# Pooled attention and routed experts in one program: where a later batch's products, a split tile's sums and the last tiles' sums stand in the TensorE queue

## The chip, the cores and the metric

The kernel runs on one core of a Trainium2 chip. The metric is the time of one execution in microseconds, the median of three runs. Five engines work side by side, each through its own queue in program order: TensorE (PE, with its weight loads shown as PEld), VectorE (DVE), ScalarE (ACT), GpSimd (POOL) and SyncE (SP), which only issues transfers. A queue whose next instruction waits on a semaphore holds back all that stands behind it.

## The reference, cut to what matters

Eight batches of eight heads with 576 tokens of 64 numbers. Keys and values are averaged over groups of eight tokens, so that each query sees 72 pooled keys. The result, 4608 tokens of 512 numbers, goes to a router and eight experts; each expert takes exactly 576 tokens, in the order of the largest logits.

```python
k_p = k.reshape(B, H, Sp, pool, D).mean(axis=3)
v_p = v.reshape(B, H, Sp, pool, D).mean(axis=3)
scores = scale * np.matmul(q, k_p.transpose(0, 1, 3, 2))
attn = np.exp(scores - np.max(scores, axis=-1, keepdims=True))
attn = attn / (np.sum(attn, axis=-1, keepdims=True) + 1e-09)
out = np.matmul(attn, v_p)
...
logits = x @ w_gate
order = np.argsort(-logits.flatten())
for idx in order:                      # the first free expert that a token's logits lead to
    tok, e = (int(idx) // E, int(idx) % E)
    if assigned[tok] >= 0 or counts[e] >= cap: continue
    assigned[tok] = e; counts[e] += 1
...
out[mask] = np.maximum(x[mask] @ w1[e], 0.0) @ w2[e]
```

## The kernel before, in words

**Attention.** The 4608 tokens are 36 tiles of 128. Since a batch has 576 tokens, four and a half tiles, four tiles (4, 13, 22 and 31) are split: their two halves belong to two batches. The order of the instructions is the order in which the Python code is written; nothing moves them afterwards. The loop of `run` goes over n = 0 to 35 and works on three tiles at once:

- `st_s(n)`, L230: the scores of tile n into the PSUM tile `pss`, of which there is one (two banks).
- `st_e(n-1, g)`, L259 and L260: the exponentials `e` of tile n-1 are transposed on TensorE (three blocks for g = 0 into `pse`, two for g = 1 into `rt`), and ScalarE copies them to `eT`. `rt` is one single bank, shared with everything in `prep_v`, `prep_g` and the router.
- `st_av(n-2, g)`, L272: the products of `eT` with `vblk`, the pooled values laid out by heads, into one of two PSUM tiles `psa`. In one go they give, per head, 64 sums, eight logit parts (the value rows times the router's weights, put beside the values) and the sum of the exponentials: 73 columns. An unsplit tile has six instructions for g = 0 and four for g = 1 (each matmul of 32-bit numbers is two), a split one twelve and eight with half the columns of weights.
- `softmax(n)`, L240 to L242: maxima and subtraction on VectorE, the exponential on ScalarE.
- `norm(n-3)`, L293 to L306: reciprocals of the sums, the logits (for four tiles at a time, L299, when n-3 is the last of four), and the normalised rows `xt` on VectorE; ScalarE issues their store to `xd` in memory (L311).

GpSimd pools the keys and values of a later batch meanwhile (L175 to L198; `vsum` is written at L190). Before a batch's values can be used, `prep_v(b)` (L211, three transposes of `vsum` into `rt`, copied by ScalarE, L213) and `prep_g(b)` (L220, products with the router's weights into `rt`; VectorE writes them into `vblk`, L221) must run. They are planned in `at`, a table by n whose entries run at the end of an iteration, behind `norm`.

**The last tiles.** `finish` brings tiles 33 to 35 to their logits and starts the router: `after` is the generator `Routing.begin`, and each `next(after)` emits a piece of it between the attention's instructions. `st_av` is called with nine columns (the logits and the sum), and the 64 other columns are left to `st_x` (L281), whose twenty instructions for the last two tiles stand between the pieces of the router's search. `put_x` scales them on ScalarE (L348).

**The router.** `search` finds, in four rounds, the logit at which the first expert is full. A round compares (DVE, L631), counts on TensorE (36 small products, L636), decides on VectorE (L694) and spreads the decision (L701, L703). `close` then turns the choice into the rows of the first expert (L775), GpSimd gathers those rows (L1042, an indirect transfer), and the experts' stage begins. `warm` is a number of products of ones that nobody reads (L529). `wake` gathers 32 rows that nobody reads (L1188); one stands behind tile 30's `norm`, one in the last round of the search.

## Time and profile before

| | |
|---|---|
| median of 3 runs | 609.79 us (609.03 to 609.95) |
| the profiled execution | 609.97 us |
| its span on the chip | 608.2 us |
| mean granted TensorE clock | 0.977 |
| TensorE busy | 588.5 us, 97% of the span |
| VectorE, ScalarE, GpSimd busy | 394.1, 302.2, 175.6 us |
| attention loop | 8.6 us to 133.1 us |
| last tiles and router, up to the first gather | 133.1 us to 156.7 us |
| experts | from 160.1 us |

How to read it: times in the trace are microseconds from the start of the span. The chain that ended last is followed back from the last instruction, at each step to what released it, so what stands in it sets the end. "issue" in it is time in which an engine waited for nothing that the profile shows. In a timeline row stand the start, the duration, the engine, the line and the tiles; in brackets the idle time before it and what ended it. The granted clock is the TensorE clock as a share of full speed.

### The profile page before, as it was taken

What the parts mean: (1) busy time and instruction counts of PE and PEld (TensorE: products, weight loads), DVE (VectorE), ACT (ScalarE), POOL (GpSimd) and SP (SyncE); (2) the same over time, 40 slices, a digit from 0 to 9 for tenths busy, and PEclk for the clock granted to TensorE, in tenths of its full rate; (3) what the DMA queues carried; (4) which work ended last, traced back from release to release, by engine and by line L of the source; (5) the groups of instructions that cost most, each with busy time, mean ns of one, the idle gap of its engine ahead of it and who ended that gap; (6) DMA issues with size and microseconds to landing.
All of it is one profiled execution on the core that took longest, in us unless ns stands there. A gap on an engine that the chain in (4) does not pass through costs nothing.

```text
span 608.2 us, 11352 instructions
## 1 busy us (share of the span) xinstructions
PE 588.5 (97%) x4196; PEld 510.5 (84%) x4196; DVE 394.1 (65%) x1150; ACT 302.2 (50%) x621; POOL 175.6 (29%) x220
## 2 busy tenths in 40 slices
PE   8999999998899999999999999999999999999993
PEld 5999999987598779878977997898799889879972
DVE  7577777986796777867964886387567437506200
ACT  7444444442362275365764495267338627825210
POOL 2999999000300420221122211212121121220021
PEclk9999999995799999999999999999999999999998
DMA  9999972121550761557721942473085247313010
GB/s 356 420 423 401 420 267 86 72 87 37 160 197 1 233 173 72 190 134 224 207 71 52 337 80 62 161 242 92 36 300 134 61 162 240 87 60 148 3 57 27
DMA packets 63907, 99.87 MB, mean 164 GB/s; under 512 B 34753, under 2 KB 34785, under 8 KB 61153
## 3 DMA queue, kind: packets, MB, share of 16 engines
q1 hardware_dynamic: 52560, 70.66, 34.6%
q0 software_dynamic: 5952, 18.90, 9.1%
q10 hardware_dynamic: 5328, 9.48, 4.2%
q8 instruction: 35, 0.57, 0.4%
q14 instruction: 32, 0.25, 0.1%
HBM read 72.41 MB, written 18.87 MB: 150 GB/s over the span
## 4 chain that ended last, share of the span: by engine, by line
PE 84%; issue 8%; DVE 2%; ACT 2%; DMA 2%; POOL 1%; POOLq 0%; another core or an unknown queue 0%; ACTq 0%
PE h L1129 30%; PE h L1163 24%; PE psa L272 8%; PE pss L230 6%; PE h L1168 4%; PE pse L259 2%; PE rt L259 1%; DMA xg<-xd,rows 1%; PE rt L220 1%; PE rt L675 1%; PE rt L636 1%; PE rt L529 1%; DMA out_dram<-yt,rows 1%; POOL out_dram L1143 1%; PE rt L211 1%
## 5 line engine op out<-in xcount | busy, mean ns | idle before, releaser
L1163 PE MATMUL h<-w2l,hh 128*128 128x512 f32 x256 | 101.5, 397 | 0.0
L1163 PE MATMUL h<-w2h,hl 128*128 128x512 f32 x256 | 101.4, 396 | 0.0
L1163 PE MATMUL h<-w2h,hh 128*128 128x512 f32 x256 | 101.1, 395 | 0.3 <-PEq L1228 0.3
L1129 PE MATMUL h<-xl,w1h 128*128 128x256 f32 (+2 forms) x516 | 93.7, 300 | 0.0
L1134 ACT ACTIVATE hh<-h 128x256 fp32r<-128x256 f32 (+2 forms) x129 | 52.9, 411 | 81.7 <-PE h L1129 81.2
L1129 PE MATMUL h<-xh,w1h 128*128 128x256 f32 (+2 forms) x516 | 93.2, 299 | 0.2 <-ACT xh L1105 0.2
L1129 PE MATMUL h<-xh,w1l 128*128 128x256 f32 (+2 forms) x516 | 91.0, 297 | 0.5 <-DVE w1l L1083 0.5
L1143 POOL DMA_INDIRECT out_dram<-yt,rows x29 | 29.0, 999 | 185.7 <-ACT yt L1177 185.5
L1129 PEld LDWEIGHTS h<-xh,w1h 128*128 128x128 f32 x516 | 76.0, 189 | 3.3 <-issue 2.3
L1129 PEld LDWEIGHTS h<-xl,w1h 128*128 128x128 f32 x516 | 77.0, 190 | 0.1
L1129 PEld LDWEIGHTS h<-xh,w1l 128*128 128x128 f32 x516 | 76.1, 189 | 0.7 <-DVE w1l L1083 0.7
L1137 DVE SCALAR_TENSOR_TENSOR hl<-h,hh 128x256 fp32r<-128x256 f32 (+2 forms) x129 | 57.4, 448 | 25.6 <-ACT hr L1136 18.0
L1042 POOL DMA_INDIRECT xa<-xd,rows x33 | 32.6, 987 | 135.3 <-ACT xg L1059 51.4
L1177 ACT ACTIVATE yt<-h 128x512 f32<-128x512 f32 x32 | 19.2, 601 | 103.2 <-PE h L1163 72.6
L272 PE MATMUL psa<-vblk,eT 128*128 128x146 f32 (+5 forms) x400 | 61.9, 302 | 0.0
L1072 DVE TENSOR_TENSOR xl<-xg,xh 128x512 fp32r<-128x512 f32 (+1 forms) x33 | 20.7, 628 | 56.3 <-ACT xh L1071 56.2
L1163 PEld LDWEIGHTS h<-w2h,hh 128*128 128x128 f32 x256 | 48.2, 188 | 9.4 <-issue 0.7
L1163 PEld LDWEIGHTS h<-w2l,hh 128*128 128x128 f32 x256 | 48.3, 189 | 8.8
L1163 PEld LDWEIGHTS h<-w2h,hl 128*128 128x128 f32 x256 | 48.2, 188 | 8.8
L272 PEld LDWEIGHTS psa<-vblk,eT 128*128 128x128 f32 (+1 forms) x400 | 52.2, 182 | 1.7 <-POOL tk L175 0.3
L1083 DVE TENSOR_TENSOR w1l<-raw,w1h 128x512 fp32r<-128x512 f32 x64 | 41.4, 686 | 9.3 <-ACT w1h L1079 8.8
L1092 DVE TENSOR_TENSOR w2l<-raw,w2h 128x512 fp32r<-128x512 f32 x64 | 43.1, 680 | 2.8 <-ACT w2h L1089 2.7
(222 smaller groups left out, 962.4 us busy)
## 6 DMA issues: line engine op xcount, KB each, us to landing
raw<-in_moe_w_dram SPq DMA_DIRECT2D x64, 512.0 KB, 6.5
xd<-xt ACTq DMA_DIRECT2D x36, 256.0 KB, 4.6
rawv<-in_v_dram SPq DMA_DIRECT2D x7, 1280.0 KB, 13.9
rawk<-in_k_dram SPq DMA_DIRECT2D x7, 1152.0 KB, 13.1
rawq<-in_q_dram SPq DMA_DIRECT2D x7, 1152.0 KB, 11.6
rawk<-in_k_dram SPq DMA_DIRECT2D x2, 576.0 KB, 4.4
rawv<-in_v_dram SPq DMA_DIRECT2D x1, 768.0 KB, 7.8
rawq<-in_q_dram SPq DMA_DIRECT2D x1, 640.0 KB, 8.9
```

The lines of the kernel that those rows point to most:

```text
L230: nc.tensor.matmul(ps[cols, j // 2, 144 * (j % 2):144 * (j % 2) + 144], self.q_of(b, j, n, cols.stop - cols.start), self.kblk[b % 4][:, j] ...
L272: self.nc.tensor.matmul(o[h], self.eT[i][:, c, h], self.vblk[b % 4][:, self.BLOCKS[c]:self.BLOCKS[c + 1], cols], start=(c == cs[0]), stop= ...
L1042: self.nc.gpsimd.indirect_dma_start(out=to[:n], out_offset=None, in_=self.xd, in_offset=bass.IndirectOffsetOnAxis(ap=rows[:n, t:t + 1], ax ...
L1072: later(0.9, 0.7, lambda: self.nc.vector.tensor_tensor(xl, x, xh.bitcast(F32), op=OP.subtract))
L1083: self.nc.vector.tensor_tensor(l, raw, h.bitcast(F32), op=OP.subtract)
L1092: self.nc.vector.tensor_tensor(self.w2l[:, i], self.raw2[e][:, i], self.w2h[:, i].bitcast(F32), op=OP.subtract)
L1129: nc.tensor.matmul(ps[:, :m], a[:, j, fs], b[:, j, o], start=(n == 0), stop=(n == 11))
L1134: nc.scalar.activation(hh[:, f, o], ps[:, :m], AF.Relu)
L1137: later(0.65, 0.4, lambda f=f, o=o, m=m, ps=ps: nc.vector.scalar_tensor_tensor(hl[:, f, o], ps[:, :m], 0.0, hh[:, f, o].bitcast(F32), op0= ...
L1143: st = nc.gpsimd.indirect_dma_start(out=rows, out_offset=bass.IndirectOffsetOnAxis(ap=idx, axis=0), in_=y, in_offset=None)
L1163: nc.tensor.matmul(ps, a[:, f, o], b[:, f], start=(f == 0 and k == 0), stop=(f == 7 and k == 2))
L1168: nc.tensor.matmul(ps[64 * a:64 * a + 64, :256], self.hr[:, f], self.raw2[e][:, f, 256 * a:256 * a + 256], start=(f == 0), stop=(f == 7))
```

## The change

- `prep_v` and `prep_g` leave the table `at`. They are called directly behind `st_s(n)`, in the same iterations as before (`prep_v(b)` in n = first[b], `prep_g(b)` in the next; for batch 1 one iteration later each, n = 5 and 6).
- In an iteration whose `st_av` is of a split tile, both `st_e` come first and then both `st_av`. For unsplit tiles the order stays.
- `finish` computes the sums of the last two tiles whole, 73 columns, and `st_x` and `put_x` go. Tile 34's sums go into `pss` in place of `psa`, and their first part stands ahead of tile 35's transposes. The rows `xt` of tiles 33, 34 and 35 are all scaled on ScalarE at the end (24 instructions; before, 16, and one on VectorE for tile 33).
- The second `wake`, the three `warm` products in the first `close` and the last three double steps of `begin` go. What those steps emitted is now emitted by the experts' stage, with nothing of the attention between.

```diff
-    def st_av(self, i, g, cols=slice(0, 73)):
+    def st_av(self, i, g, bank=("psa", 2)):
         if g == 0:
-            self.pA[i] = self.ps.tile([128, 2, 512], F32, name="psa", bufs=2)
+            self.pA[i] = self.ps.tile([128, 2, 512], F32, name=bank[0], bufs=bank[1])
...
-        gate = slice(64, 73)
-        self.st_e(j, 0)
-        self.st_av(i, 0, gate)
-        self.st_e(j, 1)
-        self.st_av(i, 1, gate)
-        self.norm(i - 1)
+        self.st_av(i, 0, ("pss", 1))
+        for g in range(2):
+            self.st_e(j, g)
+        self.st_av(i, 1)
+        rinv = {i - 1: self.gates(i - 1, i - 1, i)}
         next(after)
...
+        for g in range(2):
+            self.st_av(j, g)
+        for t in (i, j):
+            if t == j:
+                next(after)
+            rinv[t] = self.gates(t, t, t + 1)
+            next(after)
+        for t in (i - 1, i, j):
+            ps = self.sums_of(t)
+            xt = self.wk.tile([128, 8, 64], F32, name="xt", bufs=8)
+            for h in range(8):
+                self.nc.scalar.activation(xt[:, h], ps[:, h, :64], AF.Copy, scale=rinv[t][:, h:h + 1])
+            self.store(t, xt)
...
-            plan(first[b] + (b == 1), self.prep_v, b)
-            if b > 1:
-                plan(first[b] + 1, self.prep_g, b)
+            behind[first[b] + (b == 1)] = lambda b=b: self.prep_v(b)
+            behind[first[b] + 1 + (b == 1)] = lambda b=b: self.prep_g(b)
...
-            if n >= 1:
-                self.st_e(n - 1, 0)
-            if n == first[1] + 2:
-                self.prep_g(1)
-            if n >= 2:
-                self.st_av(n - 2, 0)
-            if n >= 1:
-                self.st_e(n - 1, 1)
+            if n in behind:
+                behind[n]()
+            e = [lambda g=g: self.st_e(n - 1, g) for g in range(2 if n >= 1 else 0)]
+            av = [lambda g=g: self.st_av(n - 2, g) for g in range(2 if n >= 2 else 0)]
+            if n >= 2 and len(self.parts(n - 2)) == 1:
+                e[1:1] = av[:1]
+                av = av[1:]
             if n == 1:
-                self.prep_v(0)
-            if n >= 2:
-                self.st_av(n - 2, 1)
+                e.append(lambda: self.prep_v(0))
+            for f in (*e, *av):
+                f()
             self.softmax(n)
...
-                if not spare:
-                    self.wake()
...
-        if not k:
-            self.warm(3)
...
         self.best(self.NC - 1, self.NC)
         next(g)
         yield
-        for _ in range(3):
-            next(g)
-            next(g)
-            yield
```

On TensorE, in the iterations n = 9 and 10, where batch 2 is prepared (a row is the line, the instruction, the tile written and those read; `x2` means two such instructions in a row):

```order
 L259 MATMUL rt<-ident,e 127x128 x2
 L272 MATMUL psa<-vblk_178,eT_172 128x2x73 x2
-L211 MATMUL rt<-ident,vsum 128x128 x3
 L230 MATMUL pss<-kblk_132,rawq 128x144 x4
+L220 MATMUL rt<-wblk,vT 128x40
+L220 MATMUL rt<-wblk,vT 128x32
+L220 MATMUL rt<-wblk,vT 128x16
 L259 MATMUL pse<-ident,e 127x128 x3
```

The transposes of `vsum` no longer stand between the last sums of iteration 9 and the scores of tile 10 (they now stand behind tile 9's scores, one iteration's length earlier), and the products with the router's weights stand right behind tile 10's scores.

On TensorE, around the split tile 13 (iteration n = 15, the first rows are the end of n = 14):

```order
 L259 MATMUL rt<-ident,e 127x128 x2
 L272 MATMUL psa<-vblk_179,eT_171 128x2x73 x2
-L220 MATMUL rt<-wblk,vT 128x40
-L220 MATMUL rt<-wblk,vT 128x32
-L220 MATMUL rt<-wblk,vT 128x16
 L230 MATMUL pss<-kblk_133,rawq 128x144 x4
 L259 MATMUL pse<-ident,e 127x128 x3
+L259 MATMUL rt<-ident,e 127x128 x2
 L272 MATMUL psa<-vblk_179,eT_172 64x2x73
 L272 MATMUL psa<-vblk_180,eT_172 64x2x73
```

The second pair of transposes, which stood behind the first twelve products of the split tile, moves ahead of them, so that all twenty products stand in a row.

On TensorE, behind the loop. Before, with nine columns per head:

```order
L272 MATMUL psa<-vblk_180,eT_171 128x2x73 x2
L259 MATMUL pse<-ident,e 127x128 x3
L272 MATMUL psa<-vblk_180,eT_172 128x2x9
L272 MATMUL psa<-vblk_180,eT_172 128x3x9
L272 MATMUL psa<-vblk_180,eT_172 128x2x9
L259 MATMUL rt<-ident,e 127x128 x2
L272 MATMUL psa<-vblk_180,eT_172 128x2x9 x2
L272 MATMUL psa<-vblk_180,eT_173 128x2x9
L272 MATMUL psa<-vblk_180,eT_173 128x3x9
L272 MATMUL psa<-vblk_180,eT_173 128x2x9 x3
```

and with the change:

```order
L272 MATMUL psa<-vblk_180,eT_171 128x2x73 x2
L272 MATMUL pss<-vblk_180,eT_172 128x2x73
L272 MATMUL pss<-vblk_180,eT_172 128x3x73
L272 MATMUL pss<-vblk_180,eT_172 128x2x73
L259 MATMUL pse<-ident,e 127x128 x3
L259 MATMUL rt<-ident,e 127x128 x2
L272 MATMUL pss<-vblk_180,eT_172 128x2x73 x2
L272 MATMUL psa<-vblk_180,eT_173 128x2x73
L272 MATMUL psa<-vblk_180,eT_173 128x3x73
L272 MATMUL psa<-vblk_180,eT_173 128x2x73 x3
```

Here `eT_172` is tile 34 and `eT_173` tile 35. The first products of tile 34 move ahead of tile 35's transposes and into `pss`, and all have 73 columns per head; the rows of L281, which followed between the counting products, are gone.

## The prediction

> **What bounds the kernel now.** I read the chain that ended last first: TensorE holds 84% of it, and through the attention loop it runs from one TensorE group to the next almost without a gap. A group of products that takes less time on TensorE there therefore moves the end. Rows of the chain (start, duration, what), around the preparation of batch 3 and the split tile 13, with one row of batch 1 and one of an ordinary iteration:

> ```profile
> PE 84%; issue 8%; DVE 2%; ACT 2%; DMA 2%; POOL 1%; POOLq 0%; another core or an unknown queue 0%; ACTq 0%
> ...
> 25.11 0.98 PE pss L230 x8
> ...
> 29.98 0.58 PE rt L220 x6
> ...
> 49.80 1.10 PE pss L230 x8
> ...
> 56.11 0.12 issue
> 56.23 0.52 PE rt L211 x3
> 56.75 0.98 PE pss L230 x8
> 57.73 0.33 PE pse L259 x3
> 58.06 0.87 PE psa L272 x6
> 58.94 0.22 PE rt L259 x2
> 59.16 0.50 PE psa L272 x4
> 59.66 0.03 issue
> 59.69 0.84 PE rt L220 x6
> 60.53 1.08 PE pss L230 x8
> ...
> 62.96 0.42 PE rt L259 x2
> ```

> The reader is to see two prices of the same work. Three transposes cost 0.33 us where nothing is in their way (L259) and 0.12 + 0.52 us for `prep_v` (L211); six products with the router's weights cost 0.58 us in batch 1 and 0.03 + 0.84 us in batch 3. Both stand right behind `st_e(n-1, 1)`, whose bank `rt` they need: they wait for ScalarE's copy of it and then pay the pipeline's start.

> Behind the loop the path changes hands between TensorE and VectorE. Timeline rows of the last tiles and of the router's four rounds:

> ```profile
> 133.66 0.60 PE L259 MATMUL pse<-ident,e 128*127 128x128 f32 x3 [0.60 <-ACT e L242]
> ...
> 134.54 0.68 DVE L306 TENSOR_TENSOR xt<-psa,rinv 128x512 f32<-128x512 f32 x1
> ...
> 134.99 2.18 PE L272 MATMUL psa<-vblk,eT 128*128 128x18 f32 x14
> ...
> 135.25 0.38 ACT L260 ACTIVATE eT<-rt 127x256 f32<-127x256 f32 x1 [0.36 <-PE rt L259]
> ...
> 137.21 0.21 DVE L293 RECIPROCAL rinv<-psa 128x8 f32<-128x8 f32 x1
> ...
> 138.26 1.86 PE L281 MATMUL pss<-vblk,eT 128*128 128x128 f32 x6
> ...
> 138.52 0.22 DVE L631 TENSOR_TENSOR cmp<-q16a,j 128x128 bf16<-128x128 f16 x1
> ...
> 140.05 0.29 PE L636 MATMUL rt<-oh,cmp 128*32 128x8 bf16 x4
> ...
> 141.29 0.90 DVE L631 TENSOR_TENSOR cmp<-q,j 128x256 bf16<-128x256 f16 x3
> ...
> 141.85 1.75 ACT L348 ACTIVATE xt<-pss,rinv 128x64 f32<-128x64 f32 x8 [6.22 <-DVE cmp L631]
> ...
> 142.17 1.36 PE L636 MATMUL rt<-oh,cmp 128*32 128x8 bf16 x36
> ...
> 144.47 0.89 DVE L631 TENSOR_TENSOR cmp<-q,j 128x256 bf16<-128x256 f16 x3
> ...
> 145.57 1.36 PE L636 MATMUL rt<-oh,cmp 128*32 128x8 bf16 x36
> ...
> 147.86 0.90 DVE L631 TENSOR_TENSOR cmp<-q,j 128x256 bf16<-128x256 f16 x3
> ...
> 148.20 1.36 PE L636 MATMUL rt<-oh,cmp 128*32 128x8 bf16 x36 [0.23 <-DVE cmp L631]
> ```

> Counting (L636) starts 0.34 us after the comparison where nothing stands between (147.86 to 148.20), but 0.88 us after it in the second round, 1.10 us in the third, and the first round's last count waits until L281 is through, though its comparison ended at 138.74.

> **The change part by part.** *Preparation behind the scores.* Behind `st_s(n)` the bank `rt` has long been copied, and ScalarE copies `vT` while TensorE goes on with `st_e(n-1, 0)` and `st_av`. I take 0.33 us for the transposes and 0.58 us for the products, as in the rows. Before, they cost 0.12 + 0.52 + 0.03 + 0.84 = 1.51 us, less 0.12 us since scores behind `prep_v` take 0.98 us and not 1.10. The gain is 1.39 - 0.91 = 0.48 us a batch, 2.9 us for batches 2 to 7. The bounds: nothing, if the pipeline's start is paid at the new place, and 3.5 us.

> Two things are given back. The products end in a VectorE instruction (L221) that now stands ahead of tile n's maxima:

> ```profile
> 25.56 0.86 POOL L190 TENSOR_TENSOR vsum<-t 128x320 f32<-128x320 f32 x1
> ...
> 44.03 0.76 DVE L240 TENSOR_REDUCE mx<-pss 128x8 f32<-128x576 f32 x1 [0.96 <-PE pss L230]
> ...
> 46.60 0.68 DVE L306 TENSOR_TENSOR xt<-psa,rinv 128x512 f32<-128x512 f32 x1
> ...
> 47.20 0.24 DVE L221 TENSOR_TENSOR vblk<-rt,mask 128x88 f32<-128x88 f32 x1
> ```

> From the maxima's start to the end of `xt` VectorE needs 3.25 us in an iteration that also sums four tiles' logits (n = 10 here, and n = 14). The maxima would start 0.58 + 0.07 + 0.24 = 0.89 us after the scores, so `xt` ends 4.1 us after them. TensorE wants that `psa` at 0.58 + 0.33 + 0.87 + 0.22 + 0.50 + 1.10 + 0.33 = 3.9 us. It waits 0.2 us in batches 2 and 3; in batch 7, where the router's first pieces load VectorE too, I allow as much: 0.6 us in all. The exponentials themselves are not late: maxima, subtraction and ScalarE take about 2.4 us from the maxima's start, so they are there at 3.3 us against 3.6 us. If that margin is gone, a batch loses what it gained (rival B). And in batch 1 `vsum` is done at 26.42 us, while tile 5's scores end at 26.09 us: 0.33 us lost against the 0.12 us saved, 0.2 us.

> *Sums of a split tile in a row.* In iteration 15 the second transposes cost 0.42 us between two runs of half-width products, 0.22 us otherwise. In the new order TensorE changes between the widths once less: 0.20 us in four iterations, 0.8 us. The loop gives 2.9 + 0.8 - 0.6 - 0.2 = 2.9 us.

> *Whole sums of the last tiles.* The loop's last products end at 133.07 us, and TensorE then idles 0.60 us for tile 35's exponentials. With `pss` free (its last reader, the subtraction, is done before the exponential), tile 34's first part fills that time: 0.87 us to 133.94, transposes 0.33 + 0.22, then 0.50 + 0.87 + 0.50 us: 136.4 us. Before, the fourteen narrow products ended at 137.17. So whole sums are not later, at full clock; VectorE saves tile 33's `xt` (0.68 us) as well and could reach tile 35's reciprocal at 136.5. But a new wait stands there: `rinv` has two buffers, and the third one wanted (tile 35's) must wait until ScalarE has scaled tile 33 out of the first. ScalarE copies transposes until about 135.3 (0.3 us sooner than the row at 135.25 plus 0.38), and eight scalings take 1.75 us: 137.1 us, against 137.21 before. From there to the end of the comparison are 1.53 us (137.21 to 138.74), so counting starts near 138.7 and not at 140.05: 1.4 us. Bounds: 0.5 us, if the sums run at half clock, and 1.8 us without the wait. Behind the reciprocal are queued everything of VectorE's search, so that wait is on the path.

> *No products between the counts.* The second and third round lose 0.88 - 0.34 = 0.54 us and 1.10 - 0.34 = 0.76 us: 1.3 us gained. The fourth has no such gap. The sums' 24 scalings take 5.3 us of ScalarE, from 135.3 to about 141, and the last store starts then, long before the gather.

> *Wake and warm products.* These rows carry them, the next point and the rivals:

> ```profile
> 134.00:136.00 2.00, 2.00 (x21) 2.00 (x19) 1.90 (x9) 0.88 (x2) 0.00 (x0) 0.97 0.35 131
> 158.00:160.00 2.00, 1.58 (x4) 0.30 (x2) 1.96 (x4) 1.12 (x2) 1.70 (x2) 0.55 0.68 164
> ...
> 149.41 0.88 POOL L1188 DMA_INDIRECT norow<-in_moe_w_dram,noindex  x1 [41.48 <-DVE noindex L534]
> ...
> 155.15 4.43 PE L529 MATMUL h<-ones 128*128 128x512 bf16 x10
> ...
> 156.67 0.98 POOL L1042 DMA_INDIRECT xg<-xd,rows  x1 [6.38 <-issue]
> ```

> The second wake came after 41.48 us of idle GpSimd and took 0.88 us, less than the gather's 0.98: no sign of a queue gone cold, so I cost its removal at nothing, between -0.7 us (the gather may start sooner) and +0.9 us (it starts that much later again than its rows). The three warm products ran while TensorE waited for VectorE; they cost nothing.

> *Sum.* 2.9 + 1.4 + 1.3 = 5.6 us. The expert stage behind the gather keeps its order and moves whole. 609.97 - 5.6 = 604.4 us in terms of the profiled execution, which lay 0.18 us above the median: **604.2 us**.

> **The clock.** The window rows (columns: window, length, busy time of PE, PEld, DVE, ACT, POOL, then granted clock) show the clock at half from 135.9 (0.97 over 134 to 136) to 159.8 (0.55 over 158 to 160), 23.9 us. The ten warm products brought it back just before the gathered rows came. Shifted by 5.6 us they run from 149.55 to 154.0 us. [...]

> **The rivals.** *A, the forecast*, 604.2 us, 0.50.

> *B, the loop gives nothing*: VectorE's delayed maxima make TensorE wait for what it saves. For it: VectorE is busy three quarters of the loop. Against: 0.3 us of margin above. Only 2.7 us remain: 607.1 us, 0.15.

> [...] Price: 2 to 3.4 us at half clock, 1.0 to 1.7 us: 605.5 us, 0.14.

> *D, better*: the gather loses its 0.7 us of delay and the first counts run before the clock falls: 602.8 us, 0.09.

> *E, the other side*: without the three warm products the clock stays at half through the first expert's pieces. Place: TensorE from 154 us on. Price: half of the time spent so. It decides from 6.8 us lost (5.6 plus what can be told), 13.6 us at half clock: 611.0 us. For it: the half clock lasted 23.9 us with TensorE mostly busy. Against: ten warm products alone brought it back. 0.07. [...]

> *F, a cold GpSimd queue*: the gather pays what the second wake took on itself, its 0.88 us, a landing like the gather's 3.3 us, and 0.9 us of late start, 5.1 us: 609.3 us, 0.05. Against it stands the row at 149.41. [...]

> **How the numbers follow.** A measurement here tells 0.2%, 1.2 us, from no change. A, B, C and D are faster (0.88), F the same (0.05), E slower (0.07). The range leaves out E, F and a little of A and B: the low end is D with 1 us more from the loop's bounds (2.9 to 3.5 us and the new wait's 0.4), 601.8; the high end B with half a microsecond of late gather, 607.6.

> **What would show it.** Right: L211 and L220 with about 0.33 and 0.58 us in the chain and no "issue" ahead of them; the loop's last products ending near 130.2; VectorE's last reciprocal waiting for ScalarE; L636 starting 0.34 us after each comparison; the gather near 151. Wrong: DVE or ACT ahead of L230 or L272 in the chain of the loop (B); half clock beyond 154 (C, E); the gather more than 1 us behind its rows (F).

## The result, and the profile after

The changed kernel takes 603.46 us (median of 4 runs, 603.16 to 603.46), against 609.41 us for the kernel before on the same chip (608.62 to 609.95). The ratio is 0.9895, 95% interval 0.9882 to 0.9908. The forecast was 604.2 us with a range of 601.8 to 607.6, faster with 0.88. The profiled execution after took 603.46 us with a span of 601.6 us, 6.5 us less than the profiled one before.

The page of the kernel after, shares of the chain that ended last by engine:

```profile
PE 80%; issue 7%; DVE 5%; DMA 2%; ACT 2%; POOL 1%; POOLq 0%; another core or an unknown queue 0%; SPq 0%; ACTq 0%; DVEq 0%
```

TensorE lost four points of the path, VectorE gained three: part of the loop is now bound by VectorE.

To size the loop without its first tiles, take VectorE's row maxima, one instruction a tile, as mile marks. Timeline of the kernel before, the maxima of tiles 7 and 35 (start, duration, engine, line, instruction):

```profile
34.33 0.76 DVE L240 TENSOR_REDUCE mx<-pss 128x8 f32<-128x576 f32 x1 [0.34 <-PE pss L230]
...
131.07 0.74 DVE L240 TENSOR_REDUCE mx<-pss 128x8 f32<-128x576 f32 x1
```

The same two marks of the kernel after:

```profile
34.39 0.76 DVE L240 TENSOR_REDUCE mx<-pss 128x8 f32<-128x576 f32 x1
...
127.53 0.74 DVE L240 TENSOR_REDUCE mx<-pss 128x8 f32<-128x576 f32 x1
```

Between the marks lie 96.74 us before and 93.14 us after: the loop gave **3.60 us**. From tile 35's maxima to the first gather the time fell from 25.60 to 22.73 us, **2.87 us**. What lies ahead of tile 7 cost 0.06 us, and the rest of the span, with what lies around it, gave 0.1 us: 6.5 us in all. Eight profiles of kernels with the changed loop read 93.10 to 93.26 us between the marks, so differences of a few tenths mean something there.

The chain of waits of the kernel after, around the preparation of batches 2 and 3 and the split tile 13 (start, duration, what):

```profile
43.75 0.57 PE rt L220 x6
44.32 0.44 PE pse L259 x3
...
44.85 0.50 ACT eT L260
...
45.38 0.76 DVE e L241
...
47.18 0.61 DVE xt L297
...
47.92 1.11 PE psa L272 x6
...
53.83 0.48 PE rt L211 x3
...
57.22 0.57 PE rt L220 x6
57.79 0.43 PE pse L259 x3
...
61.24 0.22 PE rt L259 x2
61.46 1.52 PE psa L272 x20
```

The reader is to see three things. The products (L220) cost 0.57 us and no "issue" stands ahead of them, as forecast; the group behind them pays 0.10 us of it back (0.43 against 0.33 us), which the forecast had left out. In batch 2 the path leaves TensorE over the exponential and VectorE and returns with `xt`, whose bank the sums wait for: the give-back that the forecast named. In batch 3 nothing of the kind stands there. The split tile's twenty products run in one piece of 1.52 us behind transposes of 0.22 us (1.02 and 0.65 us in two pieces before, with the 0.42 us between them).

What the bank has to do with it can be read from the products' waits. Kernel before, batches 2 to 7, the products of L220:

```profile
L220 PE MATMUL rt<-wblk,vT x36: 262/276/303, 46.0 to 122.9; 128*128 128x40 f32 x12, 128*128 128x32 f32 x12, 128*128 128x16 f32 x12
its engine sat idle before it (us, times) until:
  ACT eT L260: 1.5, 6
```

In each of the six batches TensorE waited for ScalarE's copy out of `rt`, 1.5 us together; the same view of the kernel after has no wait at all. For the transposes (L211) the profile names no such wait, so there the bank's part is argued from the order.

The timeline of the kernel after, from the last tiles to the first gather:

```profile
128.86 0.67 PE L272 MATMUL psa<-vblk,eT 128*128 128x146 f32 x4
...
129.37 1.03 PE L272 MATMUL pss<-vblk,eT 128*128 128x146 f32 x6
...
131.53 1.75 ACT L324 ACTIVATE xt<-psa,rinv 128x64 f32<-128x64 f32 x8
...
133.31 0.21 DVE L284 RECIPROCAL rinv<-psa 128x8 f32<-128x8 f32 x1
...
134.90 0.29 PE L604 MATMUL rt<-oh,cmp 128*32 128x8 bf16 x4 [0.68 <-DVE cmp L599]
...
136.13 0.90 DVE L599 TENSOR_TENSOR cmp<-q,j 128x256 bf16<-128x256 f16 x3
136.48 1.36 PE L604 MATMUL rt<-oh,cmp 128*32 128x8 bf16 x36 [0.88 <-DVE cmp L599]
...
138.78 0.90 DVE L599 TENSOR_TENSOR cmp<-q,j 128x256 bf16<-128x256 f16 x3
139.13 1.36 PE L604 MATMUL rt<-oh,cmp 128*32 128x8 bf16 x36 [0.87 <-DVE cmp L599]
...
149.12 0.17 DVE L739 TENSOR_SCALAR rows<-found 128x5 int32<-128x5 int16 x1
...
150.26 0.98 POOL L1002 DMA_INDIRECT xg<-xd,rows  x1 [42.11 <-DMA raw<-in_moe_w_dram]
```

The loop's last products end at 129.53 us here (the first row; tile 34's first products start just ahead of that), at 133.07 before. Tile 35's reciprocal comes 3.78 us behind that (4.14 before), right behind ScalarE's scaling of tile 33, and the first round's last count 5.37 us (6.98 before). Each later count starts 0.35 us behind its comparison (0.88 and 1.10 us before). From the loop's end to the gather are 20.73 us, 23.60 before: 2.87 us, where the forecast had 1.4 + 1.3. Not all of it is the work of the edits behind the loop (experiment 3).

The clock, windows of the kernel after (window, length, busy time of PE, PEld, DVE, ACT, POOL, then the granted clock and the DMA):

```profile
136.00:138.00 2.00, 1.36 (x36) 1.38 (x37) 1.57 (x9) 1.72 (x8) 0.00 (x0) 0.86 0.35 131
...
150.00:152.00 2.00, 2.00 (x8) 0.69 (x6) 1.30 (x3) 1.46 (x3) 1.44 (x2) 0.72 0.55 195
```

Around the first of these the clock reads 1.00 (134 to 136 us) and 0.50 (138 to 140), around the second 0.50 (148 to 150) and 1.00 (152 to 154). A clock that goes from 1.00 to 0.50 inside a window of 2 us leaves a mean of 0.86 if it falls at 137.44; 0.72 if it rises at 151.12. By this working half clock lasted 13.7 us, against 23.9 before, and the first gathered rows met full clock in both.

### The profile page after: what moved, and what is told of

It reads as the page before. It is cut to its first block, busy times and chain, and to the rows that moved or that the text cites. A ratio compares the mean times of both kernels' runs of the same rounds, so it can differ in the third digit from the quotient of the medians.

```text
span 601.6 us, 11310 instructions
## 1 busy us (share of the span) xinstructions
PE 578.2 (96%) x4173; PEld 505.1 (84%) x4173; DVE 393.2 (65%) x1148; ACT 303.0 (50%) x629; POOL 174.7 (29%) x219
## 4 chain that ended last, share of the span: by engine, by line
PE 80%; issue 7%; DVE 5%; DMA 2%; ACT 2%; POOL 1%; POOLq 0%; another core or an unknown queue 0%; SPq 0%; ACTq 0%; DVEq 0%
PE h L1089 30%; PE h L1123 24%; PE psa L272 7%; PE pss L230 6%; PE h L1128 4%; PE pse L259 2%; DMA xg<-xd,rows 1%; PE rt L259 1%; PE rt L503 1%; PE rt L641 1%; DVE e L241 1%; PE rt L604 1%; PE rt L220 1%; POOL out_dram L1103 1%; DMA out_dram<-yt,rows 1%
## 5 line engine op out<-in xcount | busy, mean ns | idle before, releaser
L1089 PE MATMUL h<-xl,w1h 128*128 128x256 f32 (+2 forms) x516 | 93.7, 300 | 0.0
L1089 PE MATMUL h<-xh,w1h 128*128 128x256 f32 (+2 forms) x516 | 93.2, 299 | 0.2 <-issue 0.2
L1089 PE MATMUL h<-xh,w1l 128*128 128x256 f32 (+2 forms) x516 | 91.0, 297 | 0.5 <-DVE w1l L1043 0.5
L1089 PEld LDWEIGHTS h<-xh,w1h 128*128 128x128 f32 x516 | 76.1, 190 | 3.3 <-issue 2.8
L1089 PEld LDWEIGHTS h<-xl,w1h 128*128 128x128 f32 x516 | 77.0, 190 | 0.1
L1089 PEld LDWEIGHTS h<-xh,w1l 128*128 128x128 f32 x516 | 76.1, 190 | 0.7 <-DVE w1l L1043 0.7
L1002 POOL DMA_INDIRECT xa<-xd,rows x33 | 32.5, 986 | 135.3 <-ACT xg L1019 51.0
L272 PE MATMUL psa<-vblk,eT 128*128 128x146 f32 (+3 forms) x390 | 59.3, 301 | 0.1
L272 PEld LDWEIGHTS psa<-vblk,eT 128*128 128x128 f32 (+1 forms) x390 | 50.8, 179 | 1.5 <-issue 0.3
```

Source lines behind the costliest of these rows:

```text
L272: self.nc.tensor.matmul(o[h], self.eT[i][:, c, h], self.vblk[b % 4][:, self.BLOCKS[c]:self.BLOCKS[c + 1]], start=(c == cs[0]), stop=(c == ...
L1002: self.nc.gpsimd.indirect_dma_start(out=to[:n], out_offset=None, in_=self.xd, in_offset=bass.IndirectOffsetOnAxis(ap=rows[:n, t:t + 1], ax ...
L1089: nc.tensor.matmul(ps[:, :m], a[:, j, fs], b[:, j, o], start=(n == 0), stop=(n == 11))
```

## The experiments

All times are medians, with the ratio to the kernel before on the same chip. Experiments 1 to 4, 5 to 8 and 9 to 12 ran on a chip each. The kernel before read 609.3, 609.9 and 609.8 us there, so medians of different groups can lie about half a microsecond apart without any edit.

**1. The preparation back at its place.**

```diff
-            behind[first[b] + (b == 1)] = lambda b=b: self.prep_v(b)
-            behind[first[b] + 1 + (b == 1)] = lambda b=b: self.prep_g(b)
+            plan(first[b] + (b == 1), self.prep_v, b)
+            if b > 1:
+                plan(first[b] + 1, self.prep_g, b)
...
+            if n == first[1] + 2:
+                e.insert(1, lambda: self.prep_g(1))
```

> The changed kernel with the preparation of a later batch's products put back to where it stood (behind the exponentials' second transposes and the sums), all else as changed. Forecast's theory: the new place is worth 0.48 us in each of six batches less 0.8 us given back, so the time rises by about 2.1 us, to 605.6 us. The changed kernel's trace read piece by piece (0.70 us in batch 1, 0.12, 0.56, 0.51, 0.55, 0.66 and 0.13 us in batches 2 to 7, of which the split tiles' own order has some): about 2.5 us, 606.0 us. Rival B (the loop gives nothing, the gain is all behind it): no change, 603.5 us. The products behind tile scores go back to 0.84 us and the transposes to 0.52 us in the chain. A rise of less than 1.2 us would speak for B.

Measured 606.17 us (605.70 to 606.63), ratio 0.9944 (0.9931 to 0.9958): 2.7 us slower than the changed kernel. Its timeline, the two marks:

```profile
34.77 0.76 DVE L240 TENSOR_REDUCE mx<-pss 128x8 f32<-128x576 f32 x1
...
130.62 0.75 DVE L240 TENSOR_REDUCE mx<-pss 128x8 f32<-128x576 f32 x1
```

95.85 us lie between them, 2.71 us more than in the changed kernel: the new place is worth that much beside the split tile's new order, and 2.46 us beside the old order (96.74 before against 94.28 in the next experiment). Rival B is out. One number of the expectation is out as well: the 0.70 us put down to batch 1. This kernel's tile 7 comes 0.4 us later than in either kernel, not because of its order but because a load of queries landed late (tile 4's scores waited 0.71 us for it); what happens ahead of tile 7 is not the change's doing alone (experiments 9 and 10).

**2. A split tile's sums in the old order.**

```diff
-            if n >= 2 and len(self.parts(n - 2)) == 1:
+            if n >= 2:
```

> The changed kernel with the old order of a split tile's sums (first transposes, first sums, second transposes, second sums) and nothing else put back. Forecast's theory: 0.20 us in each of four iterations, plus 0.8 us, 604.3 us. The traces' theory: each split tile gained 0.33 us (twenty products in 1.53 us against 1.02 and 0.65 us, transposes 0.22 against 0.42 us), plus 1.3 us, 604.8 us. Rival: the preparation's new place and the split tile's order help one another, since batch 3 to 6 have the split tile in the iteration ahead and lost none of their gain to late maxima, where batch 2 without a split tile did: then the old order brings such waits to batches 3 to 6 and the rise is above 2 us.

Measured 604.65 us (604.45 to 606.07), ratio 0.9929 (0.9914 to 0.9943): 1.2 us. The marks:

```profile
34.32 0.76 DVE L240 TENSOR_REDUCE mx<-pss 128x8 f32<-128x576 f32 x1 [0.34 <-PE pss L230]
...
128.60 0.74 DVE L240 TENSOR_REDUCE mx<-pss 128x8 f32<-128x576 f32 x1
```

94.28 us, 1.14 us more than the changed kernel, with three split tiles (13, 22, 31) between the marks: 0.38 us each. Without the preparation's move the same order gives 96.74 - 95.85 = 0.89 us, 0.30 each. The two edits help one another by 0.25 us; the rise above 2 us that the rival wanted did not come.

**3. The loop's edits alone**, on the kernel before: the changed `run` and the old `finish`, wake and warm products.

```diff
+            if n in behind:
+                behind[n]()
...
+            if n >= 2 and len(self.parts(n - 2)) == 1:
+                e[1:1] = av[:1]
+                av = av[1:]
```

> The kernel before with the loop's two edits alone (preparation behind the scores, a split tile's sums in a row); the last tiles' narrow sums, the products between the counts, the second wake and the three warm products stay as before. Forecast's theory: the loop gives 2.9 us, 606.5 us. The traces' theory: the loop gives 4.5 us less what the start's phase does, 605.0 us, and the rest from the loop's end to the gather stays 23.6 us long. Rival B: no gain, 609.4 us. [...]

Measured 606.38 us (605.35 to 606.77), ratio 0.9948 (0.9934 to 0.9962): 3.0 us of gain, the forecast's 2.9. Between the marks lie 93.10 us (34.29 to 127.39), as in the changed kernel. The expectation that the rest would stay as long as before was missed: from tile 35's maxima to the gather the profile reads 25.08 us, 0.52 less than in the kernel before, though nothing was edited there. The narrow sums of the last tiles were that much shorter:

```profile
131.32 1.64 PE L272 MATMUL psa<-vblk,eT 128*128 128x18 f32 x14
```

They took 2.18 us in the kernel before, whose clock fell at 135.9 us, in their midst; here it fell at 132.84 us by the same working (0.71 over 132 to 134 us), when they were all but through. So the two profiled executions differ by 4.2 us where the medians differ by 3.0; this one, at 605.80 us, was one of the two quicker ones of five. Where the slower ones lost time no profile shows; the first tiles (experiments 9 and 10) are the likely place. From here to the changed kernel are 606.38 - 603.46 = 2.9 us (the kernel before read the same within 0.1 us on both occasions): the share of the other edits, where the forecast had 2.7; between the two profiles the way from tile 35's maxima to the gather gives 2.35.

**4. The second wake and the three warm products kept.**

```diff
+                if not spare:
+                    self.wake()
...
+        if not k:
+            self.warm(3)
```

> The changed kernel with the second wake of the GpSimd queue and the three warm products kept as before. Forecast's theory: both cost nothing and give nothing, 603.5 us within 0.5 us. Rival F (the removed wake made the gather slow): the kept wake makes it faster, by the up to 0.9 us that it took itself. [...] Rival D (the wake delayed the gather): 0.7 us slower.

Measured 603.34 us (603.21 to 603.49), ratio 0.9900 (0.9885 to 0.9915): no difference. The gather came 0.94 us behind its rows (150.16 against 149.05 + 0.17), 0.97 without them. Half clock lasted 13.6 us with them, 13.7 without. Removing them neither cost nor gave anything; rivals F, E and D's earlier gather fall.

**5. Three buffers for the reciprocals.**

```diff
-        rinv = self.wk.tile([128, 8], F32, name="rinv")
+        rinv = self.wk.tile([128, 8], F32, name="rinv", bufs=3)
```

> The changed kernel with three buffers for the reciprocals instead of two, so that the last tile's reciprocal need not wait for ScalarE's scaling of tile 33. Forecast's theory: the wait costs 0.4 us on the path (137.1 against 136.7 us without it), so 603.1 us. The trace of the changed kernel: VectorE is free for it at 133.17 us and TensorE's sums are done at 133.06, and it ran at 133.31, so 0.14 us and no more: 603.3 us; the first round's last count comes 0.14 us sooner after the loop's end. If the distance from the loop's end to the reciprocal stays at 3.94 us, the wait was never ScalarE's.

Measured 604.05 us (603.90 to 604.83), ratio 0.9897 (0.9854 to 0.9939), which cannot tell tenths on another chip. The timeline can:

```profile
130.03 1.03 PE L272 MATMUL pss<-vblk,eT 128*128 128x146 f32 x6
...
133.76 0.21 DVE L284 RECIPROCAL rinv<-psa 128x8 f32<-128x8 f32 x1
...
135.35 0.29 PE L604 MATMUL rt<-oh,cmp 128*32 128x8 bf16 x4 [0.47 <-DVE cmp L599]
```

The reciprocal comes 3.73 us behind the start of tile 34's first products instead of 3.94, the last count 5.32 instead of 5.53 (3.95 and 5.54 in experiment 9, which has two buffers). The wait that the forecast named is real and cost 0.21 us, half of its 0.4.

**6. Batch 2's products one iteration later.**

```diff
-            behind[first[b] + 1 + (b == 1)] = lambda b=b: self.prep_g(b)
+            behind[first[b] + 1 + (b in (1, 2))] = lambda b=b: self.prep_g(b)
```

> The changed kernel with the six products for batch 2 one iteration later (behind tile 11's scores instead of tile 10's). Iteration 10 sums four tiles' logits on VectorE; iteration 11 does not. Theory of the late maxima (the forecast's 0.2 us given back in batch 2): the chain no longer crosses VectorE between 44.8 and 47.9 us and batch 2 gains 0.5 us instead of the 0.1 us it gained, so 603.1 us, and tile 11's maxima come some 0.35 us sooner after tile 7's. Rival: what batch 2 lacks is a wait for its pooled values, which moves along: no change, 603.5 us, and the gap of about 0.35 us stands in iteration 11 or 12.

Measured 603.85 us (603.80 to 604.03), ratio 0.9890 (0.9848 to 0.9932). Its chain at the new place:

```profile
47.40 0.57 PE rt L220 x6
47.98 0.43 PE pse L259 x3
48.40 0.01 issue
48.41 1.11 PE psa L272 x6
```

The detour over VectorE is gone from the path, so the late maxima were the cause. But from tile 9's to tile 11's maxima the time only fell from 7.14 to 6.99 us: 0.15 us, close to the forecast's 0.2 and not the 0.35 of the expectation (to tile 13's maxima, with the products inside the stretch in both kernels, it fell from 13.32 to 13.16 us). The sums still pay 1.11 us for six products here, 0.87 elsewhere, though nearly no wait is left.

**7. No ten warm products ahead of the gathered rows.**

```diff
-    warm(10)
```

> The changed kernel without the ten warm products ahead of the first gathered rows (they compute nothing). [...] The forecast's rival E (the clock stays at half while the expert's pieces wait for one another): plus 6.8 us, 610.3 us. If the first expert is bound by its gathers and not by TensorE: no change, 603.5 us.

Measured 607.12 us, ratio 0.9946 (0.9926 to 0.9966), in two groups: three runs from 604.99 to 605.54 and seven from 606.89 to 607.67. Windows of its profile:

```profile
136.00:138.00 2.00, 1.34 (x36) 1.32 (x37) 1.60 (x8) 1.75 (x8) 0.00 (x0) 0.92 0.35 131
...
160.00:162.00 2.00, 2.00 (x13) 2.00 (x12) 1.19 (x3) 0.60 (x1) 0.00 (x0) 0.60 0.30 63
```

By the same working the clock fell at 137.68 and rose at 161.60 us: 23.9 us, as in the kernel before. The first expert's pieces ran from 153.8 to 161.6 us at half clock: four products of L1089 (128x256) took 0.85 us there (160.75 to 161.60) and 0.48 us behind the rise. The median lies 3.2 us above experiments 5 and 6 on the same chip, which is more than rival C's price for a later return of the clock, 1.0 to 1.7 us, and less than E's 6.8 us. The two groups lie 2.0 us apart, with a mean granted clock of 0.975 in the seven and 0.978 to 0.979 in the three. The half-clock stretches of the profiles lie 3.4 us apart (last section); 3.4 us more at half clock would cost 1.5 us by the two durations of L1089, an estimate. The profile is of one of the seven, so where the clock turned in the three is not shown. By the record TensorE was busy without a gap from 153.77 us on, and yet the clock came back only 7.8 us later. In the kernel after it came back 2.4 us behind the start of the ten warm products (148.71), in the kernel before 4.6 us (155.15). How much busy time brings it back is not shown.

**8. Tile 34's sums in one of the loop's two banks.**

```diff
-        self.st_av(i, 0, ("pss", 1))
+        self.st_av(i, 0)
```

> The changed kernel with tile 34's sums in one of the two banks of the loop instead of the scores' bank. Theory: those sums then wait until VectorE has read tile 32's sums (its scaled values end in the last iteration), and the last tile's sums wait for tile 33's readers: ScalarE's eight scalings, which stand behind both last tiles' reciprocals. The order of the scalings makes this wait 1.5 to 2.5 us: 605.0 to 606.0 us. Rival: TensorE idles there for the last tile's exponentials anyway and the wait is hidden but for 0.2 to 0.6 us: 603.7 to 604.1 us.

Measured 607.01 us (606.85 to 607.25), ratio 0.9945 (0.9929 to 0.9961): 3.1 us above experiments 5 and 6. Its chain behind the loop:

```profile
130.88 0.12 DVE rinv L284
...
131.03 1.11 PE psa L272 x6
...
133.33 1.64 ACT xt L324 x8
...
135.02 1.66 PE psa L272 x10
...
136.76 0.22 DVE rinv L284
```

Two waits in a row: tile 34's first sums wait 1.03 us for VectorE's readers of the older bank, and tile 35's sums for all eight scalings of tile 33 on ScalarE. The reciprocal of tile 35 comes at 136.76, 3.45 us later than in the changed kernel, in a profile whose loop ran 0.47 us later: 3.0 us. The other bank is what makes whole sums at the end worth having: without it the ratio is 0.9945, no better than the loop's edits alone (0.9948).

**9. The changed kernel again**, with the three that follow on the same chip.

> The changed kernel once more, as the reference of the three kernels run with it on the same chip. All theories: 603.4 to 604.1 us (ratio 0.990), with the first scores somewhere between 8.2 and 9.5 us and a wait of batch 1's transposes for GpSimd's sums that differs with it.

Measured 603.92 us (603.83 to 604.17), ratio 0.9905 (0.9888 to 0.9921). Its chain of waits in the first tiles:

```profile
26.57 0.87 POOL vsum L190
...
27.48 0.55 PE rt L211 x3
```

Here the path to the end runs through GpSimd's pooling of batch 1, and TensorE waited 1.04 us for it. In the changed kernel's first profile it waited 0.01 us: TensorE reached that place 0.34 us later (by tile 5's maxima, 26.82 against 26.48) and GpSimd's last sum began 0.69 us sooner (25.88).

**10. Batch 1's transposes back at the end of their iteration.**

```diff
-            behind[first[b] + (b == 1)] = lambda b=b: self.prep_v(b)
+            if b == 1:
+                plan(first[b] + 1, self.prep_v, b)
+            else:
+                behind[first[b]] = lambda b=b: self.prep_v(b)
```

> The changed kernel with batch 1's transposes alone back at the end of their iteration; its products and the other batches stay as changed. Forecast's theory: at the new place they wait 0.2 us for GpSimd's sums; going back gains 0.2 us and pays 0.1 us: 603.4 us. Traces of eight kernels: at the new place TensorE waits 0.0, 0.24, 0.28, 0.55, 0.61, 0.61, 0.0 and 1.07 us there, by how early its first scores came; going back takes the wait away and keeps the order of the rest, so the median falls by 0.3 to 0.6 us: 603.0 us, with tile 6's maxima some 4.3 us after tile 5's in every profile. Rival: the wait only moves to the next thing that GpSimd delivers (the values' blocks, 2.6 us behind the sums, or batch 2's keys): no change, 603.5 us.

Measured 604.16 us (603.56 to 604.72), ratio 0.9907 (0.9890 to 0.9923). No gain. In its profile the wait for the sums is gone, but tile 4's scores waited 0.95 us for a load of queries, and the products lost 0.27 us to ScalarE's copy. Tile 7 came at 35.51 us, later than in any other profile. The load's wait stands ahead of the edited place, so it is not the edit's doing, and the rival (the wait moves to what GpSimd delivers next) did not show either. What the edit does is seen from tile 5's to tile 7's maxima. With batch 1's transposes at the end and the new order of the split tile, three profiles read 7.95 to 7.99 us; with them at the new place, nine read 7.57 to 8.63, 8.10 on average, and what they have above 7.57 us is the wait for GpSimd's sums (0.81 us of wait make 8.37, 1.04 make 8.61). For batch 1 the new place gains 0.4 us when GpSimd is early, loses as much or more when it is late, and loses 0.1 us on average. Why GpSimd and the loads deliver at other times from one execution to the next stays open.

**11. A row gather ahead of the first gather.**

```diff
             X.load_1(R.eid, 0, 4 if p else 2)
+            if not p:
+                X.xg0 = X.buf("xg", [128, 5, 512])
+                nc.gpsimd.indirect_dma_start(out=X.xg0[:32, 0], out_offset=None, in_=xd,
+                    in_offset=bass.IndirectOffsetOnAxis(ap=R.ti[:32, 0:1], axis=0))
```

> The changed kernel with one more row gather ahead of the first expert's first gather: it reads a fixed row of the same source into the same buffer and is overwritten. So the twelve semaphores that the first gather waits for are waited for some 8 us sooner, and the first gather itself waits for two. Theory of the semaphores: the first gather started 0.95 to 0.97 us behind its rows in every trace so far, later ones 0.25 us, because GpSimd's queue goes through those waits one by one; it now starts 0.25 to 0.3 us behind its rows and everything after it 0.7 us sooner, 602.8 us. Rival: it started 0.07 to 0.10 us behind the landing of the first expert's first load in the five traces where both were read; if that landing releases it, it starts there again and nothing changes, 603.5 us. Rival on the clock: the gather comes sooner but the first pieces meet half clock for longer, 603.2 us.

Measured 603.83 us (603.39 to 604.20), ratio 0.9901 (0.9885 to 0.9918): 0.1 us better than the changed kernel beside it, not told apart. Its timeline:

```profile
149.92 0.17 DVE L739 TENSOR_SCALAR rows<-found 128x5 int32<-128x5 int16 x1
150.36 1.01 POOL L1003 DMA_INDIRECT xg<-xd,rows  x1 [6.83 <-DVE rows L739]
...
153.82 1.02 PE L1064 MATMUL tp<-ident,xg 128*128 128x128 f32 x4
...
155.53 0.66 PE L1090 MATMUL h<-xh,w1h 128*128 128x128 f32 x4 [0.25 <-ACT xh L1066]
```

The gather starts 0.27 us behind its rows, and ahead of the landing of the first expert's first load (151.10 us here). So that landing, which the profile names for the changed kernel (the row at 150.26 above), is not what releases it. The waits hold the gather back, but their number does not count as the expectation had it. Between the rows, done at 155.72 us, and the gather the chain of the kernel before shows:

```profile
155.81 0.04 POOLq L1042
...
155.90 0.04 POOLq L1042
155.94 0.73 issue
```

These are two separate waits for two semaphores each, all long due, and then 0.73 us until the gather starts. The changed kernel has the same two at 149.37 and 149.46 us. Of its twelve semaphores six had been passed as they came due, from 126.6 to 135.7 us, and the seventh is that of the rows; five are left behind the rows, as in the kernel before. In this experiment nothing is left. Why the start behind the separate waits takes 0.73 us, and 0.27 us behind the rows alone, stays open.

Then the gain shrinks. Against experiment 9 the gather starts 0.66 us sooner (150.36, 151.02) and the transposes 0.52 us (153.82, 154.34), but they take 1.02 instead of 0.81 us, since the clock came back at 154.64 in this profile. The first pieces start 0.30 us sooner (155.53, 155.83), and the rows of expert 2 come at 243.96 against 244.03 us. 0.2 us went to the clock; where the last 0.2 us went within the first two experts was not followed.

**12. Four edits together** (5, 6, 10 and 11).

> The changed kernel with four edits together: batch 1's transposes at the end of their iteration, batch 2's products one iteration later, three buffers for the reciprocals, and the gather ahead of the first one. If they add up: 0.4 + 0.15 + 0.2 + 0.7 = 1.45 us, 602.0 us. If the first gather hangs on the load's landing: 602.7 us. [...]

Measured 602.93 us (602.65 to 603.20), ratio 0.9888 (0.9871 to 0.9904): 1.0 us below the changed kernel on the same chip, and no run of the one lies within the runs of the other. This version beats both kernels. In its profile tile 7 came 0.39 us sooner than in experiment 9, the first gather 1.37 us sooner, the rows of expert 2 1.20 us, and the clock returned at 151.04 against 154.68 us. How much of the 1.0 us is the edits' own and how much the clock's return, 3.64 us earlier, the runs don't separate.

## Why the prediction was right

The sign and the size held, and so did the mechanism in the main; the median lies 0.7 us from the forecast. That the loop's 2.9 us met the median's 3.0 so closely is luck in part, as the terms show:

*Preparation behind the scores.* The forecast was 0.48 us for each of six batches, 2.9 us, less 0.6 us for late maxima in batches 2, 3 and 7: 2.3 us. Measured alone 2.46 us, beside the split tile's new order 2.71. What the prediction calls the pipeline's start is in the kernel before's timeline: three transposes behind a running group (L259 at 57.57) begin 0.16 us ahead of that group's end, so that 0.33 of their 0.49 us fall behind it; behind a wait (L211 at 56.23) all 0.52 us do. The price of L220 held (0.57 us for 0.58), but the transposes behind it pay 0.10 us more in every batch, a cost that the forecast did not have. The price of L211 held in batches 2, 4 and 6 (0.33 us) and not behind a split tile's scores (0.48 us in batches 3 and 5). The give-back was real in batch 2 (0.15 us by experiment 6) and again in the last iterations, where the path now runs over VectorE; in batch 3 it did not come.

*The split tile's sums.* Mis-sized: 0.20 us a tile in the forecast, 0.30 to 0.38 measured. The forecast counted the second transposes alone (0.42 to 0.22 us) and left out that the twenty half-width products take 1.52 us in one piece and 1.67 us in two.

*Batch 1.* A net loss of 0.2 us in the forecast, 0.1 us on average in the profiles (experiment 10), so the size was about right, but it was put as one number. The wait on `vsum`, 0.33 us in the forecast, read 0, 0.01, 0.24, 0.28, 0.55, 0.61, 0.61, 0.81, 1.04 and 1.07 us in ten profiles of kernels with the new place, 0.52 on average. The forecast had set the end of GpSimd's sums in one trace against TensorE's time in the same trace, and neither is fixed.

*The loop's sum.* Between the marks the forecast's terms give 2.9 us (2.9 for six batches, 0.6 for three split tiles, less 0.6), and 3.60 us were measured: 0.7 too little. By the medians the loop's edits gave 3.0 us. What the slower executions lost is not shown, so that 2.9 met 3.0 is not the forecast's merit alone.

*Behind the loop.* 1.4 + 1.3 us forecast, 2.87 measured against the kernel before and 2.35 against experiment 3, where the clock fell behind the narrow sums. The steps are those named: the last count no longer behind L281 (1.61 us and 1.08 us in the two comparisons), and 0.53 and 0.75 us off the second and third rounds. The forecast's 1.4 us lies between the two; it did not reckon with the place at which the clock falls. The bound for whole sums at half clock was not tried: in no profile with whole sums did the clock fall ahead of their end (137.44 against 133.06 us in the kernel after). The new wait for ScalarE's scaling took 0.21 us on the path, not 0.4. And the whole sums needed their banks: with the loop's own two this part would have taken 3 us longer (experiment 8).

*Wake and warm products* at nothing: right (experiment 4).

*Rivals.* B fell with experiments 1 to 3, although the sign that the prediction gave for it, VectorE or ScalarE ahead of L230 or L272 in the chain, did come, in batch 2 and in the last iterations; the sign was too broad. C and E lean on the same cause, a later return of the clock. In the changed kernel's first profile it came at 151.12 us, in its second at 154.68, so C's later return does occur; it did not take the result off the forecast. The upper end of C's price, 3.4 us at half clock, was shown by no run when it was set; the two profiles' half-clock stretches, 13.7 and 17.0 us, do lie 3.4 us apart. E's price was set by 13.6 us of half clock; without any warm products the first expert's pieces met 7.8 us of it. F and D's early gather had the same wrong premise, that the wake has a say in the gather's 0.95 us: it is 0.94 us with the wake and 0.97 without (experiment 4), and 0.27 us when the older waits are passed ahead of time (experiment 11).

## What to carry to other kernels

Work that a bank ties to the instruction just ahead of it cost less here behind a group that leaves that bank alone (0.57 us for 0.84, 0.33 for 0.52), and the gain could be read in advance from the same work elsewhere in the trace, to 0.10 or 0.15 us, by which the price changed with the neighbours; so could what an edit gives back (0.2 us forecast, 0.15 measured in batch 2), by adding up what the next engine in turn has still to do before its result is wanted. Where an edit asks for data earlier, put its price as a range over several profiles: the moment at which a load or GpSimd delivers was the least steady number here (waits of 0 to 1.07 us for the same sums). And look at the waits of the first instruction that writes memory which earlier work used: here the first gather carried twelve semaphores, and a throw-away gather ahead of time took them off its start. That was 0.7 us at the gather, of which the program's time showed no more than 0.1.
